# The first attention chunk's scores: products in the layout of the projection, summed over the head dimension by column-tiled matmuls

## The chip, the cores and the metric

The kernel runs on one core of a Trainium2 chip. The metric is the device time of the core in microseconds (us). A profile's own span is about 1.8 us shorter than the time of the same execution. Engines: TensorE (PE in the profile; PEld is its weight loads), VectorE (DVE), ScalarE (ACT), GpSimd (POOL), SyncE (SP).

Before the change: 777.38 us, the median of three executions (777.25 to 777.75).

## The reference

One transformer block on 2048 rows of 1024 features. Cut to what matters:

```python
def attention_part(x, wqkv, wo):           # H = 32 heads of Dh = 32, window W = 8, dilation 2
    q, k, v = split_heads(x @ wqkv)
    idx = pos[:, None] - 2 * arange(8)      # each position sees itself and 7 earlier ones, two apart
    logits = einsum("bhsd,bhswd->bhsw", q, k[idx]) * Dh ** -0.5
    attn = softmax(where(idx >= 0, logits, -1e9))
    return merge_heads(einsum("bhsw,bhswd->bhsd", attn, v[idx])) @ wo

h  = x + attention_part(layernorm(x), wqkv, wo)
n  = layernorm(h)
h2 = h + ((n @ w_gate) * (n @ w_up)) @ w_down    # 3584 hidden features
```

## The kernel before

The rows are worked in four chunks of 512. For a chunk, TensorE computes q, k and v in 24 groups of eight matmuls of 512 columns (4 of 128 output features in each of six weight blocks: 0 and 1 are q, 2 and 3 k, 4 and 5 v). In that layout a partition is one feature, and the sum over the 32 features of a head runs across partitions; the additions of this kernel's VectorE all run along the free dimension. So each group's result goes to DRAM and is loaded again with a partition for every pair of a quarter of the chunk and a head:

```python
def evac_qkv(c, m, ps):
    sg = t1k.tile([128, HB + TC], BF, ...)
    nc.scalar.copy(sg[:, HB:HB + TC], ps[:])
    # ... the 14 earlier columns (the halo) for k and v ...
    nc.sync.dma_start(qd[c][...], sg[...])        # and kd, vd
```

Now the head's features lie along the free dimension, and the scores of two window positions are two products and a tree of halving adds:

```python
def attention(c):                                  # cut
    for wp in range(W // 2):
        for j in range(2):
            nc.vector.tensor_tensor(prod[:, j], qD[:], kD[:, :, o:o + SUB], ALU.mult)
            yield 2.3
        nc.vector.tensor_tensor(prod[:, :, 0:16], prod[:, :, 0:16], prod[:, :, 16:32], ALU.add)
        yield 2.3
        # ... 8, 4, 2, 1: five adds in all ...
    # ... mask, maximum, exponential, sum, reciprocal ...
    prefetch_qk(c + 1)
    while ("v", c) not in qkv_in:
        yield "later", 1.0
    # ... eight products with v ("pv") and their adds, then the store and reload of the output ...
```

The attention is a generator. A scheduler called after each matmul group decides how much of it is put into the program there. It is pure bookkeeping while the program is written, and does nothing on the chip:

```python
GROUP_US = 1.73
class Background:
    def spend(self, us):
        self.credit -= us
    def step(self, us):
        self.now += us
        self.credit = min(self.credit + us * self.rate, 4.0)
        while self.credit > 0:
            # take the first item that is ready; next(item) puts its next
            # instructions into the program and yields their cost
            self.credit -= got
```

The stretch that decides this case is the first output projection, `wo_ln2(0)`: eight groups of matmuls, whose results VectorE adds to the residual, with statistics and a normalisation for every 128 rows, which a DMA then transposes. Between it and the gate projection of the next part (`ffn1(0)`, tile `pg`), which reads all the transposed rows, lie eight groups of other work:

```python
    bg.finish(atts[0])
    bg.rate = 0.98
    nxt = wo_ln2(0)                       # per group: bg.spend(0.7 ...); bg.step(GROUP_US)
    qkv(3, range(4, 6), last=True)        # eight groups
    start_attention(3)
    lnT2, hs = nxt
    hT = ffn1(0, lnT2)                    # pg, pu
```

The order at the start of the program:

```python
    qkv(0, range(1, 4))
    load_qk(0)
    # ...
    start_attention(0)                    # ready 16 us later
    qkv(1, range(4))
    qkv(0, range(4, 6))
    load_v(0)
```

## Time and profile before

| | before |
|---|---|
| time, median of 3 | 777.38 us |
| span of the profiled execution | 774.8 us |
| TensorE busy | 768.9 us (99%) |
| VectorE busy | 612.0 us (79%) |
| TensorE's waits | 2.5 us, of which 2.1 before the first projection |

The table says that TensorE has almost no room: it is busy for 768.9 of 774.8 us. The author's estimate from this is that an added matmul makes the program longer by what it occupies, unless it falls into a wait, and that work taken off another engine makes it hardly shorter. The prediction below shows the rows. One more pair of rows is useful as the "before" of two comparisons. The first fence is TensorE in order of time (start, us, engine, line, operation, tiles, count) around the first output projection of the kernel before; the second is its DMA view of the 16 us in which the rows of a later chunk are transposed, as GB/s in 40 slices of 0.4 us.

```profile
163.33 13.98 PE L515 MATMUL wo<-w_wo,oT 128*128 128x512 bf16 x64
190.96 1.89 PE L394 MATMUL pg<-lnT,w_wg 128*128 128x512 bf16 x8
```

```profile
GB/s 314 348 344 346 293 296 288 291 288 291 288 292 293 288 289 287 276 155 261 281 291 238 217 206 169 220 204 181 179 207 202 144 216 209 154 205 206 201 150 219
```

The gate projection begins 27.6 us after the output projection, with 16 groups of 1.73 us between them: no wait. The transposes move 144 GB/s or more in every slice.

### The profile page before, as it was taken

Reading aid. Unit: us, or ns where it says so; the run is one execution under the profiler, and the core shown is the slowest. Engines: PE = TensorE matmul, PEld = TensorE weight load, DVE = VectorE, ACT = ScalarE, POOL = GpSimd, SP = SyncE. Lnnn points to the kernel's source line nnn. Section 1 sums busy time; section 2 is a strip of 40 time slices with the busy share of each in tenths; the row PEclk is TensorE's granted clock in tenths of the full one; section 3 lists DMA queues with packets and bytes.
Section 4 is the critical chain, followed back from the end, with each engine's and each line's share of the span. In section 5 each row is a group of like instructions: output and inputs, shape, how many; then the busy total and the mean of one; then the engine's idle time right before and its main releaser. Section 6 shows DMA issues by size and latency. Waiting matters only on the chain.

```text
span 774.8 us, 10428 instructions
## 1 busy us (share of the span) xinstructions
PE 768.9 (99%) x3691; PEld 353.5 (46%) x3691; DVE 612.0 (79%) x782; ACT 471.3 (61%) x1021; POOL 142.1 (18%) x152
## 2 busy tenths in 40 slices
PE   8999999999999999999999999999999999999998
PEld 6444444444444444444444444444444444444444
DVE  5629999999899999999988989985553444578863
ACT  4627534323476661975869899746677776788240
POOL 0000000010000200002000001008778687600000
PEclk9999999999999999999999999999999999999999
DMA  8998693895965868876745375644332423740001
GB/s 285 262 267 194 160 288 86 259 287 145 342 204 167 269 226 242 263 231 229 240 138 195 129 271 150 158 100 111 108 93 71 109 59 105 241 140 28 0 28 55
DMA packets 183716, 134.38 MB, mean 173 GB/s; under 512 B 81264, under 2 KB 176496, under 8 KB 181616
## 3 DMA queue, kind: packets, MB, share of 16 engines
q1 hardware_dynamic: 176912, 110.12, 49.9%
q0 software_dynamic: 3584, 22.02, 8.2%
q10 hardware_dynamic: 3168, 1.57, 0.9%
q8 instruction: 29, 0.48, 0.3%
q14 instruction: 23, 0.19, 0.1%
HBM read 104.86 MB, written 22.02 MB: 164 GB/s over the span
## 4 chain that ended last, share of the span: by engine, by line
PE 86%; DVE 9%; DMA 2%; ACT 1%; SPq 1%; issue 0%; DVEq 0%
PE ps L394 18%; PE pu L394 12%; PE pg L394 12%; PE dx L790 6%; PE pz L683 6%; PE acc L629 6%; PE py L683 6%; PE px L683 6%; PE wo L515 4%; PE pv L683 3%; PE dy L790 3%; DMA x<-in_A_x_dram 2%; DVE st L181 1%; DVE h L837 1%; PE ps L355 1%; PE ex L790 1%
## 5 line engine op out<-in xcount | busy, mean ns | idle before, releaser
L394 PE MATMUL ps<-lnT,w_qkv 128*128 128x512 bf16 x736 | 159.7, 379 | 0.2 <-ACT sg L307 0.2
L394 PEld LDWEIGHTS <-w_qkv 128*128 128x128 bf16 x736 | 71.8, 98 | 86.6 <-issue 0.7
L394 PE MATMUL pg<-lnT,w_wg 128*128 128x512 bf16 x448 | 105.8, 379 | 0.0
L394 PE MATMUL pu<-lnT,w_wu 128*128 128x512 bf16 x448 | 105.8, 379 | 0.0
L307 ACT CAST sg<-ps 128x512 bf16<-128x512 f32 x96 | 54.7, 590 | 51.3 <-PE ps L394 49.9
L477 DVE TENSOR_TENSOR pv<-vD,at 128x4096 bf16<-128x4096 bf16 x32 | 72.5, 2286 | 0.3
L434 DVE TENSOR_TENSOR prod<-qD,kD 128x4096 bf16<-128x4096 bf16 x32 | 72.3, 2284 | 0.1
L683 PEld LDWEIGHTS <-sw 128*128 128x128 f16 x448 | 43.8, 98 | 53.5 <-issue 0.9
L394 PEld LDWEIGHTS <-w_wu 128*128 128x128 bf16 x448 | 43.9, 98 | 52.8
L394 PEld LDWEIGHTS <-w_wg 128*128 128x128 bf16 x448 | 43.8, 98 | 52.7
L599 ACT CAST us<-pu 128x512 bf16<-128x512 f32 x56 | 33.2, 592 | 40.3 <-PE pu L394 39.5
L683 PE MATMUL px<-lnT,ws 128*128 128x512 bf16 x224 | 55.2, 379 | 0.0
L683 PEld LDWEIGHTS <-ws 128*128 128x128 f16 x336 | 32.9, 98 | 39.6
L629 PE MATMUL acc<-w_wd,gs 128*128 128x512 bf16 x224 | 48.5, 379 | 0.0
L489 POOL DMA_DIRECT2D od<-oD x4 | 2.2, 542 | 251.4 <-DVE oD L487 162.5
L664 POOL TENSOR_TENSOR sw<-ws 128x512 f16<-128x512 f16 x26 | 29.9, 1150 | 84.8 <-PE py L683 77.5
L185 ACT ACTIVATE rs<-mv,eps 128x1 f32<-128x1 f32 (+1 forms) x25 | 7.4, 297 | 53.5 <-DVE mv L182 48.6
L594 ACT CAST gs<-pg 128x512 bf16<-128x512 f32 x56 | 32.8, 586 | 10.7 <-PE pg L394 8.7
L436 DVE TENSOR_TENSOR prod<-prod 128x4096 bf16<-128x4096 bf16 x16 | 36.6, 2289 | 0.3
L543 ACT ACTIVATE junkd<-w_wd 128x512 bf16<-128x512 bf16 x56 | 34.3, 613 | 0.0
L629 PEld LDWEIGHTS <-gs 128*128 128x128 bf16 x224 | 21.9, 98 | 26.4
L700 ACT COPY py<-px 128x512 f32<-128x512 f32 x28 | 16.0, 570 | 26.3 <-PE px L683 26.3
(312 smaller groups left out, 1390.7 us busy)
## 6 DMA issues: line engine op xcount, KB each, us to landing
w_wg<-in_B_w_gate_dram SPq DMA_DIRECT2D x14, 1024.0 KB, 6.9
w_wu<-in_B_w_up_dram SPq DMA_DIRECT2D x14, 1024.0 KB, 5.4
w_wd<-in_B_w_down_dram SPq DMA_DIRECT2D x8, 896.0 KB, 7.7
w_pair<-in_B_w_gate_dram SPq DMA_DIRECT2D x14, 512.0 KB, 4.0
w_pair<-in_B_w_up_dram SPq DMA_DIRECT2D x14, 512.0 KB, 5.3
w_wo<-in_A_wo_dram SPq DMA_DIRECT2D x6, 1024.0 KB, 8.3
w_qkv<-in_A_wqkv_dram SPq DMA_DIRECT2D x5, 1024.0 KB, 11.0
kd<-sg SPq DMA_DIRECT2D x32, 144.0 KB, 3.3
```

What stands on the lines that cost most here:

```text
L307: nc.scalar.copy(sg[:, HB:HB + TC], ps[:])
L394: nc.tensor.matmul(ps[:], lhsT=wt[:, ko, bass.ts(j, 128)], rhs=rhs[:, ko, :], start=(ko == 0), stop=(ko == KO - 1))
L434: nc.vector.tensor_tensor(prod[:, j], qD[:], kD[:, :, o:o + SUB], ALU.mult)
L436: nc.vector.tensor_tensor(prod[:, :, 0:16], prod[:, :, 0:16], prod[:, :, 16:32], ALU.add)
L477: nc.vector.tensor_tensor(pv[:, j], vD[:, :, o:o + SUB], at[:, w, None, :].to_broadcast((128, DH, SUB)), ALU.mult)
L515: nc.tensor.matmul(ps[:], lhsT=oTs[c][:, kk, t, :], rhs=wts["wo", c, hf][:, kk, :], start=(kk == 0), stop=(kk == KO - 1))
L543: nc.scalar.activation(junk, src, ACTF.Abs, accum_out=self.l1[:, k:k + 1])
L594: nc.scalar.copy(gs[:], pg[:])
L599: nc.scalar.copy(us[:], pu[:])
L629: nc.tensor.matmul(acc[t][:], lhsT=hT[f][:, bass.ts(t, 128)], rhs=wts["wd", c, hf, b][:, j, :], start=(f == 0), stop=(f == NF - 1))
L683: nc.tensor.matmul(ps[:], lhsT=lhs[:, ko, :], rhs=rhs[:, ko, :], start=(fresh and ko == 0), stop=(ko == 3), skip_group_check=not fresh)
L790: nc.tensor.matmul(ps[:, bass.ds(lo, n)], lhsT=lhs[k][:, bass.ts(q, 128)], rhs=rhs[k][:, bass.ds(lo, n)], start=(fresh and k == 0), stop=( ...
```

## The change

For chunk 0 alone, the trip through DRAM is left out. q and k stay in the layout of the projection (`qT`, `kT`). VectorE multiplies them there, two groups of heads and four window positions in one instruction, and the sum over a head's 32 features is done by TensorE: a matmul with a weight of 128 x 32 zeros and ones adds up the partitions of each head. Its weight has 32 columns where the ordinary ones have 128 (128*32 and 128*128 in the traces), so four such matmuls, one for each quarter of the chunk, are sent to four different column tiles (quarters of the array's columns). The result lands in the layout that the rest of the attention expects. The intent is to start chunk 0's attention some 20 us earlier and to take the adding tree off VectorE. The order of the weight blocks and of the first projections is changed so that a half of q and of k are there early. Core of the diff, with cuts marked:

```diff
+NAT = (3, 2, 1, 0, 7, 6, 5, 4)
-    for b in range(6):
+    for b in (0, 2, 1, 3, 4, 5):
         stream.append((("qkv", b), wqkv_v[:, :, bass.ts(b, 512)], KO))
 # ... mask in the order NAT; "heads": the 0/1 weights; tiles qT, kT ...
     def evac_qkv(c, m, ps):
+        if c == 0 and m < 16:
+            natural.add(m)
+            # ... copy ps into qT or kT (and the halo), no DMA ...
+            return
+    def natural_logits(lg):
+        # ... four product buffers; acc: two PSUM tiles ...
+        def reduce(i):
+            for g in range(2):
+                hg = i // 2 * 2 + g
+                for cp in range(4):
+                    rows = slice(32 * cp, 32 * cp + 32)
+                    nc.tensor.matmul(acc[i % 2][rows], lhsT=heads[:, hg, :],
+                                     rhs=bufs[i % 4][:, g, :, bass.ts(cp, SUB)],
+                                     start=(hg == 0), stop=(hg == KO - 1))
+        for i in range(8):
+            # ... wait until the four groups that are needed are in "natural" ...
+            nc.vector.tensor_tensor(bufs[i % 4], qT[...].to_broadcast((128, 2, 4, TC)), win, ALU.mult)
+            yield 2.3
+            if i > 1:
+                reduce(i - 2)
+        yield "later", 2.0
+        reduce(6)
+        nc.scalar.copy(lg[:, 0:4], acc[0][:])
+        yield "later", 2.0
+        reduce(7)
+        nc.scalar.copy(lg[:, 4:8], acc[1][:])
 # ... attention(c): logits(c, lg) for c > 0, natural_logits(lg) for c == 0 ...
-        bg.add(atts[c], bg.now + (16.0 if c == 0 else 0.0))
-    qkv(0, range(1, 4))
-    load_qk(0)
+        bg.add(atts[c], bg.now)
+    qkv(0, (2,))
+    start_attention(0)
+    qkv(0, (1, 3))
```

More of the change, by code (lines that the diff above doesn't have):

```diff
@@ L295 @@
     nc.gpsimd.memset(mask[:], 0.0)
-    for w in range(1, W):
-        nc.gpsimd.memset(mask[:, w, 0:DIL * w], NEG)
+    for i, w in enumerate(NAT):
+        if w:
+            nc.gpsimd.memset(mask[:, i, 0:DIL * w], NEG)
+    heads = t1k.tile([128, KO, 32], BF, tag="t1k", name="heads")
+    nc.gpsimd.memset(heads[:], 0.0)
+    for i in range(4):
+        base = heads[32 * i:32 * i + 32, 0, i:i + 1]
+        nc.gpsimd.memset(bass.AP(base.tensor, base.offset, [list(base.ap[0]), [36, KO]]), 1.0)
+    qT = att.tile([128, KO, TC], BF, tag="qD", name="qT")
+    kT = att.tile([128, KO, HB + TC], BF, tag="kD", name="kT")
+    nc.gpsimd.memset(kT[:, :, 0:HB], 0.0)
+    natural = set()
     wps = psum.tile([128, 512], F32, tag="mm", name="warm_ps")
@@ L305, in evac_qkv @@
     def evac_qkv(c, m, ps):
+        if c == 0 and m < 16:
+            natural.add(m)
+            if m < 8:
+                nc.scalar.copy(qT[:, m, :], ps[:])
+            else:
+                nc.scalar.copy(kT[:, m - 8, HB:HB + TC], ps[:])
+                nc.scalar.copy(halo[:, m - 8, :], ps[:, TC - HB:TC])
+            return
         sg = t1k.tile([128, HB + TC], BF, tag="t1k", name=f"sg{c}_{m}")
@@ L425, in prefetch_qk, with logits @@
             load_qk(c)
-    def attention(c):
+    def natural_logits(lg):
+        room = att.tile([128, 2, 2, 4, TC], BF, tag="prod", name="nprod")
+        bufs = [room[:, 0], room[:, 1], att.tile([128, 2, 4, TC], BF, tag="oD", name="nprod_o")[:],
+                att.tile([128, 2, 4, TC], BF, tag="vD", name="nprod_v")[:]]
+        acc = [psum.tile([128, 4, SUB], F32, tag="mm", name=f"lgp{i}") for i in range(2)]
+        def reduce(i):
[3 more added lines that the diff above has]
+                    rows = slice(32 * cp, 32 * cp + 32)
+                    nc.tensor.matmul(acc[i % 2][rows], lhsT=heads[:, hg, :], rhs=bufs[i % 4][:, g, :, bass.ts(cp, SUB)],
+                                     start=(hg == 0), stop=(hg == KO - 1))
+        for i in range(8):
+            hg = i // 2 * 2
+            while not {hg, hg + 1, hg + 8, hg + 9} <= natural:
+                yield "later", 1.0
+            base = kT[:, hg, HB - DIL * (i % 2 * 4 + 3):HB]
+            win = bass.AP(base.tensor, base.offset, [list(base.ap[0]), [HB + TC, 2], [DIL, 4], [1, TC]])
+            nc.vector.tensor_tensor(bufs[i % 4], qT[:, hg:hg + 2, None, :].to_broadcast((128, 2, 4, TC)), win, ALU.mult)
+            yield 2.3
[7 more added lines that the diff above has]
+        nc.scalar.copy(lg[:, 4:8], acc[1][:])
+    def logits(c, lg):
         qD, kD = qkv_in["q", c], qkv_in["k", c]
-        lg = att.tile([128, W, SUB], F32, tag="lg", name=f"lg{c}")
         for wp in range(W // 2):
@@ L445, in attention @@
             yield 1.0
+    def attention(c):
+        lg = att.tile([128, W, SUB], F32, tag="lg", name=f"lg{c}")
+        order = range(W) if c else NAT
+        yield from logits(c, lg) if c else natural_logits(lg)
         if c == 0:
@@ L475, in attention @@
                 w = 2 * wp + j
-                o = HB - DIL * w
+                o = HB - DIL * order[w]
                 nc.vector.tensor_tensor(pv[:, j], vD[:, :, o:o + SUB],
@@ L739 @@
     bg.add(stats_gen(norm1[3]), bg.now + 6.0)
-    start_attention(0)
     qkv(1, range(4))
```

## The prediction

> **What bounds the kernel now.** I read the page's busy shares first, then TensorE's own waits, then the chain that ended last, then the order of time on VectorE. The page (engine, busy us, share, instructions):
>
> ```profile
> PE 768.9 (99%) x3691; PEld 353.5 (46%) x3691; DVE 612.0 (79%) x782; ACT 471.3 (61%) x1021; POOL 142.1 (18%) x152
> ```
>
> Busy can flatter pipelined matmuls, so I asked TensorE's list of waits (total us, times, longest us). All of it:
>
> ```profile
> PE warm_ps L301 <- DVE warm L287: 1.2, 1, 1.2
> PE pt L349 <- DVE ln L342: 0.6, 1, 0.6
> PE ps L355 <- ACT lnT L350: 0.3, 1, 0.3
> PE ps L394 <- ACT sg L307: 0.2, 1, 0.2
> PE pv L683 <- DVE h L795: 0.2, 1, 0.2
> ```
>
> TensorE waits 2.5 us in 774.8, and 2.1 of that lies before the first projection. The chain of waits (start, us, what) shows its pace and the stretch that will matter:
>
> ```profile
> 59.74 103.76 PE ps L394 x480
> 163.50 13.81 PE wo L515 x64
> 177.31 13.81 PE ps L394 x64
> 191.12 1.73 PE pg L394 x8
> ```
>
> 103.76 us over 480 matmuls is 216 ns each, though the groups show 379 ns for one: matmuls overlap, and 216 ns is the price of one more in the queue. The granted clock is 1.00 in every stretch I asked. So time is the number of TensorE slots plus its waits. Taking work off VectorE or the DMA queues saves at most the 0.2 us waits.
>
> VectorE's chain for one pair of chunk 0's window positions, in order of time (start, us, instruction):
>
> ```profile
> 59.96 4.45 DVE L434 TENSOR_TENSOR prod<-qD,kD 128x4096 bf16<-128x4096 bf16 x2
> 64.44 2.29 DVE L436 TENSOR_TENSOR prod<-prod 128x4096 bf16<-128x4096 bf16 x1
> 66.77 1.22 DVE L438 TENSOR_TENSOR prod<-prod 128x2048 bf16<-128x2048 bf16 x1
> 68.03 1.22 DVE L441 TENSOR_TENSOR t<-prod 128x1024 f32<-128x1024 bf16 x1
> 69.28 0.69 DVE L443 TENSOR_TENSOR t<-t 128x512 f32<-128x512 f32 x1
> 70.01 0.43 DVE L444 TENSOR_TENSOR lg<-t 128x256 f32<-128x256 f32 x1
> ```
>
> And the first output projection, where VectorE is late:
>
> ```profile
> 171.27 2.29 DVE L436 TENSOR_TENSOR prod<-prod 128x4096 bf16<-128x4096 bf16 x1
> 173.48 1.28 DVE L517 TENSOR_TENSOR h<-wo,h 128x512 bf16<-128x512 f32 x2
> ...
> 186.34 0.55 DVE L190 TENSOR_SCALAR ln<-h,mv,rs 128x1024 bf16<-128x1024 bf16 x1 [0.60 <-ACT rs L186]
> ```
>
> The first wo tile is on TensorE from 163.3, its add runs at 173.48; the last normalised rows are done at 186.89, their transpose lands about 3.1 us after its issue (tile lnT), near 190, and the gate projection that reads it starts at 191.0 without a wait. That chain has 1 us of slack or less.
>
> [...] No instruction of this trace is column-tiled[...]. [...] a product with a broadcast middle dimension already costs 2286 ns here (pv, L477), against 2284 ns for prod (L434).
>
> **The change part by part.**
>
> Removed: for chunk 0, 16 stores and two loads (q, k) through DRAM, and on VectorE four times the tree (2.29 + 1.22 + 1.22 + 0.69 + 0.43 = 5.85 us), 23.4 us. None is on TensorE's path: worth 0. Kept: eight products of 4096 elements, about 2.29 us each, now started near 39 us, where VectorE idles from 39.0 to 54.3.
>
> Added on TensorE: 8 reductions of 2 head groups x 4 column tiles = 64 matmuls of 512 columns, in eight separate bursts between ordinary groups. If four tiles run together, a burst is 2 rounds x 216 = 432 ns. [...] I choose 0.8 us a burst (0.45 to 1.05): 6.4 us. All of it lies on the bound.
>
> Waits for the products: following the kernel's own scheduler by its credits, reduction i is issued two products later, near 42, 46.5, 49 us and on; products end near 41.3, 43.6, 45.9 and every 2.3 us. TensorE finds them ready, by 0.7 us for the first. [...] The old 0.2 us wait at 59.7 came from ScalarE stuck behind statistics of x that landed at 54.3; these are now issued after the products, and the x loads have a freer queue, so I take that wait off: -0.2.
>
> A new wait: the attention generator runs 21 us ahead in the order of issue but VectorE executes no earlier against TensorE at wo. Its first pv now waits for v of chunk 0, whose load can't be issued before the v projections are stored (84.23 before, 5.5 us to land): about 89.6 plus the added TensorE time s. From there, with durations of before: rest of chunk 0, 34.4 (111.48 to 145.88); four score pairs of chunk 1, 41.8 (59.96 to 103.55, less 1.8 of x norms between); maximum to exponential 3.9; sum and reciprocal 2.5; at 1.2. Sum 173.4 + s for the first wo add, against 173.48: the same lateness. But the scheduler's credit now stands at -0.99 on entering wo, instead of -1.34; after the first tile's -0.70 + 1.73 it is +0.04, so one pv product of 2.28 us is put among the adds (before: -0.31, none). The last norm then comes 2.28 later relative to TensorE, -0.1 for the start, +0.2 for the missing wait, less a slack of 0 to 1: TensorE waits about 1.9 us before the gate projection.
>
> Sum: 777.4 + 6.4 + 1.9 - 0.2 = 785.5; I put 785.3, as rival (b) below is likelier than (c).
>
> **Rivals.**
>
> (a) The column tiles don't overlap. Then 64 x 216 = 13.8 us[...]: near 793 with the wo wait, just at the 2% limit (792.9). [...] For it: nothing in this trace shows tiles together. I give it 0.13.
>
> (b) No wait at wo: v lands early enough, or slack is larger: 783.5. For it: the estimate rests on sums of 90 us in which 1 us decides, and v's load may take less than 5.5 us. 0.35.
>
> (c) A larger wait: VectorE or ScalarE late in the reduction stage[...], or v landing late (the other v loads show up to 10.9 us), which would move the wo wait one for one and bring 788 to 791. 0.15.
>
> (d) The freed VectorE time shortens the kernel. The waits list allows at most 0.5 us of this. 0.01.
>
> **Range and chances.** Overlapping tiles without and with the wait give 781.0 (8 x 0.45) to 788; serial tiles or a late v reach 791 to 794. So 781 to 791.5 at 8 in 10; faster 0.01, within 2% 0.88, slower 0.11.
>
> **What would show it.** Right: new TensorE matmuls of 512 columns and 32 weights in eight bursts of about 0.8 us, their starts within a burst far closer than 216 ns; TensorE's waits list with one new entry of 1 to 3 us, at the first gate matmul (pg), released by the transpose; one pv between the first wo adds; no tree on VectorE in chunk 0. Wrong: starts 216 ns apart in a burst (rival a); a wait at a reduction for its product[...] (c); a span that is shorter with no wait removed.

## The result, and the profile after

| | before | after |
|---|---|---|
| time, median of 4 | 777.32 us | 788.76 us (787.24 to 790.25) |
| ratio | | 1.0146 (95%: 1.0132 to 1.0160) |
| span of the profiled execution | 774.8 us | 785.5 us |

A ratio here and below is the mean time of one kernel's runs over the mean of the other's runs of the same rounds, so it is not quite the ratio of the medians. 788.76 lies within the predicted range of 781.0 to 791.5, but 3.5 us above the predicted 785.3. The profiled execution of before was among the shortest seen (executions of it span 774.8 to 776.1), so differences of half a microsecond in the 10.7 between the spans aren't read further.

First the work that was taken away. The page after has for TensorE and the others (busy us, share, instructions):

```profile
PE 772.2 (98%) x3695; PEld 354.0 (45%) x3755; DVE 590.1 (75%) x762; ACT 472.8 (60%) x1015; POOL 142.0 (18%) x156
```

VectorE lost 21.9 us of work and 20 instructions. TensorE has 64 matmuls more, not the 4 that the page shows: 60 of its matmul records are missing here (the repeated run below lists all 3755, as many as weight loads). In the view by stretches, from 60 to 104 us, VectorE's busy time fell from 43.21 to 15.71 us while TensorE was busy 44.00 and 43.79 of 44.00 us: the freed time bought nothing.

Now what was added. TensorE in order of time, after:

```profile
42.71 0.61 PE L457 MATMUL lgp<-nprod,heads 128*32 128x512 bf16 x8
43.26 3.63 PE L413 MATMUL ps<-lnT,w_qkv 128*128 128x512 bf16 x16
46.81 0.61 PE L457 MATMUL lgp<-nprod,heads 128*32 128x512 bf16 x8
...
168.70 14.20 PE L569 MATMUL wo<-w_wo,oT 128*128 128x512 bf16 x63
...
199.61 1.89 PE L413 MATMUL pg<-lnT,w_wg 128*128 128x512 bf16 x8 [2.85 <-DMA lnT<-ln]
...
529.31 1.02 PE L737 MATMUL pv<-prodx,sw 128*128 128x512 f16 x4 [2.06 <-DVE h L849]
```

A burst of eight reductions begins at 42.71 and the next ordinary matmul at 43.26: 0.55 us for eight matmuls of 512 columns, where eight ordinary ones take 1.73. Between the ordinary start at 43.26 and the next burst at 46.81 lie 3.55 us, and 16 ordinary matmuls at 216 ns are 3.45: another 0.10. A burst costs 0.65 us, eight of them 5.2. No bracket at a burst: TensorE never waits for a product. The brackets at `pg` and at the late `pv` are two new waits. The list of TensorE's waits (total us, times, longest us) agrees:

```profile
PE pg L413 <- DMA lnT<-ln: 2.9, 1, 2.9
PE pv L737 <- DVE h L849: 2.3, 2, 2.1
```

Set against the same landmarks of before, the delay grows like this:

| landmark | before | after | delay |
|---|---|---|---|
| first group of 512 columns | 17.02 | 17.55 | 0.53 |
| first output projection | 163.33 | 168.70 | 5.37 |
| gate projection after it | 190.96 | 199.61 | 8.65 |
| second output projection | 287.65 | 296.30 | 8.65 |
| first `pv` of the later part | 518.67 | 529.31 | 10.64 |
| end | 774.8 | 785.5 | 10.7 |

The 10.7 us are therefore 5.2 of bursts less 0.4 of an old wait and its gap (before, the 152 matmuls from 26.54 to 59.74 took 33.2 us, and 152 x 216 ns are 32.8), 0.5 at the start, 2.85 of the wait at `pg` with 0.4 of small gaps in the output projection and behind it, and 2.1 at `pv`.

The wait at `pg` can be followed back on VectorE, in order of time:

```profile
37.30 4.49 DVE L466 TENSOR_TENSOR nprod<-qT,kT 128x4096 bf16<-128x4096 bf16 x2
...
96.88 4.50 DVE L531 TENSOR_TENSOR pv<-vD,at 128x4096 bf16<-128x4096 bf16 x2 [19.52 <-DMA vD<-vd]
...
180.71 0.68 DVE L571 TENSOR_TENSOR h<-wo,h 128x512 bf16<-128x512 f32 x1
181.31 2.28 DVE L531 TENSOR_TENSOR pv<-vD,at 128x4096 bf16<-128x4096 bf16 x1
183.51 0.68 DVE L571 TENSOR_TENSOR h<-wo,h 128x512 bf16<-128x512 f32 x1
```

The first line is the new product, 4.49 us for two, where two of the other layout took 4.45 before. VectorE then has its scores early, and at 77 us nothing to do: it waits 19.52 us for v, whose load was issued at 89.7 and took 7.1. From there on it is busy but for one wait of 1.1 us for ScalarE, and comes to the first residual add at 180.71, 12.0 us after the output projection began (10.2 before). Then one `pv` product of 2.28 us stands between the first two adds, which wasn't there before. The last rows are normalised from 195.76 to 196.31, their transpose lands 3.1 us after its issue, and the gate projection starts at 199.61; TensorE had been free for it since 196.8.

Beside this, three of the four executions after had a mean granted clock below 1.000: 0.998, 0.995 and 0.998, with spans of 786.9, 788.5 and 787.1, against 785.5 at 1.000. That is where the median lost another 1.5 us to the profiled execution.

### The profile page after: what moved, and what is told of

It is laid out like the page before. It is cut to its first block, busy times and chain, and to the rows that moved or that the text cites. A ratio compares the mean times of both kernels' runs of the same rounds, so it can differ in the third digit from the quotient of the medians.

```text
span 785.5 us, 10418 instructions
## 1 busy us (share of the span) xinstructions
PE 772.2 (98%) x3695; PEld 354.0 (45%) x3755; DVE 590.1 (75%) x762; ACT 472.8 (60%) x1015; POOL 142.0 (18%) x156
## 4 chain that ended last, share of the span: by engine, by line
PE 79%; DVE 15%; DMA 3%; ACT 1%; issue 1%; ACTq 0%; DVEq 0%
PE pg L413 12%; PE pu L413 12%; PE ps L413 8%; PE dx L844 6%; PE pz L737 6%; PE acc L683 6%; PE py L737 6%; PE px L737 6%; PE wo L889 3%; PE pv L737 3%; PE dy L844 3%; DVE pv L531 3%; DVE prod L483 2%; PE wo L569 2%; PE ex L844 2%; DVE prod L485 1%
## 5 line engine op out<-in xcount | busy, mean ns | idle before, releaser
L326 ACT CAST sg<-ps 128x512 bf16<-128x512 f32 x80 | 46.9, 588 | 64.6 <-PE ps L413 62.9
L483 DVE TENSOR_TENSOR prod<-qD,kD 128x4096 bf16<-128x4096 bf16 x24 | 54.4, 2285 | 0.1
L737 PE MATMUL px<-lnT,ws 128*128 128x512 bf16 x212 | 53.1, 379 | 0.6
L654 DVE TENSOR_TENSOR gs<-gs,us 128x512 bf16<-128x512 bf16 x56 | 23.5, 419 | 24.7 <-ACT us L653 24.5
L683 PEld LDWEIGHTS <-gs 128*128 128x128 bf16 x224 | 21.9, 98 | 26.4
L737 PE MATMUL pv<-prodx,sw 128*128 128x512 f16 x112 | 28.7, 379 | 2.3 <-DVE h L849 2.3
```

Source lines behind the costliest of these rows:

```text
L683: nc.tensor.matmul(acc[t][:], lhsT=hT[f][:, bass.ts(t, 128)], rhs=wts["wd", c, hf, b][:, j, :], start=(f == 0), stop=(f == NF - 1))
L737: nc.tensor.matmul(ps[:], lhsT=lhs[:, ko, :], rhs=rhs[:, ko, :], start=(fresh and ko == 0), stop=(ko == 3), skip_group_check=not fresh)
```

## The experiments

**Theory.** The bursts cost what they occupy. The `pg` wait comes from the order of issue (one product let in by credit) and from the late v. The late `pv` wait and the clock were not foreseen and have no reason yet. **Rivals:** the tiles don't overlap and something else became shorter; the whole loss is chip-to-chip scatter; the late wait is a consequence of the changed kernel's delay and not of its instructions.

Four experiments of three rounds, on one chip (before: 777.07).

**The changed kernel again, unaltered.**

> The changed kernel again, unaltered, for its spread and for which of its four extra costs return in a second profile (bursts 5.2 us, first-gate wait 2.9, wait at the first pv of the last stage 2.1, start 0.5). If all four belong to the change: ratio to before 1.013 to 1.016, the waits list again shows about 2.9 us at pg and about 2.1 at pv. Rival: the 2.1 and the 0.5 are chance of that one execution; then they are under 0.5 here and the span is 783 to 784.

788.13 us (786.19 to 788.39), ratio 1.0137. Both waits came back (2.8 at `pg`, and at `pv` a longest of 1.4, against 2.1), and three of four executions again had a clock of 0.998. The first group began at 17.18 instead of 17.55, so 0.2 to 0.5 us at the start is scatter. The rest repeats.

**Keep the product out by credit alone.**

```diff
     bg.rate = 0.98
+    bg.spend(0.1)
     nxt = wo_ln2(0)
```

> Changed kernel with 0.1 us of scheduler credit taken before the first output projection, so that its credit stays below zero and no pv product lands among the wo adds. My theory: one pv of 2.28 us is what made the last norm late; the wait at the first gate matmul falls from 2.9 to 0.3-0.9 us and the span by about 2.3. Rival (VectorE is late anyway, because v landed late, and the pv only fills a hole): the wait stays near 2.9 and the span unchanged.

784.69 us, ratio 1.0097. TensorE's wait list now has

```profile
PE pg L413 <- DMA lnT<-ln: 0.7, 1, 0.7
```

A tenth of a microsecond of bookkeeping moves one product and takes 2.1 us off the wait, with the same instructions executed, one of them later. The median fell by 3.4, more than the wait: the clock was 1.000, 0.999, 1.000, 1.000.

**Load v earlier.** The v projections of chunk 0 and their load are put ahead of chunk 1's q and k (and the refill of the weight stream that they need ahead of that):

```diff
     xtiles[2] = load_x(2, "x", nc.sync)
+    pump(6)
# ...
     xtiles[3] = load_x(3, "x", nc.sync)
-    pump(6)
     bg.add(stats_gen(norm1[3]), bg.now + 6.0)
-    qkv(1, range(4))
     qkv(0, range(4, 6))
     load_v(0)
+    qkv(1, range(4))
```

> Changed kernel with chunk 0's v projections moved ahead of chunk 1's q and k (and their weights loaded earlier), so that v of chunk 0 can be loaded some 28 us earlier. If VectorE's lateness at wo comes from its 19.5 us wait for v: that wait shrinks below 3 us, VectorE reaches the first wo add 6 us or more earlier against TensorE, the wait at pg is 0 and the span falls by 2.9 to 3.3 although a product is still put among the wo adds. Rival (lateness set by the number of VectorE instructions): pg still waits over 2 us. Risk: the fifth and sixth weight blocks come late and TensorE waits near 40 us.

783.30 us, ratio 1.0080; all clocks 1.000. There is no wait at `pg`. The first `pv` product ran at 75.30 without a wait, and the first residual add came 3.8 us after the output projection's start, not 12.0. VectorE still has one attention add between the residual adds, and it no longer matters. So the wait at `pg` has two causes, the product let in and the late v, and removing either all but ends it. The wait at `pv` stayed at 1.8.

**No column tiles.** The same 64 matmuls, with 0/1 weights of 128 columns that put each quarter on its own output rows, all accumulated over the full array:

```diff
-                    nc.tensor.matmul(acc[i % 2][rows], lhsT=heads[:, hg, :], rhs=bufs[i % 4][:, g, :, bass.ts(cp, SUB)],
-                                     start=(hg == 0), stop=(hg == KO - 1))
+                    nc.tensor.matmul(acc[i % 2][:], lhsT=heads[hg][:, cp, :], rhs=bufs[i % 4][:, g, :, bass.ts(cp, SUB)],
+                                     start=(hg == 0 and cp == 0), stop=(hg == KO - 1 and cp == 3))
```

> Changed kernel with the same 64 reduction matmuls at full width: 0/1 weights of 128 columns, zero outside the tile's own 32, no column tiles. If the four column tiles really run together: bursts grow from 0.55 to 1.7 us (8 x 216 ns), less about 0.1 each[...], so the span rises by 7.5 to 9 us against the changed kernel. If the tiles were not what makes the burst short: no difference over 1 us.

795.79 us, ratio 1.0242 (slower). TensorE in order of time:

```profile
18.30 7.07 PE L414 MATMUL ps<-lnT,w_qkv 128*128 128x512 bf16 x32 [0.84 <-DMA w_qkv<-in_A_wqkv_dram]
...
43.37 1.89 PE L457 MATMUL lgp<-nprod,heads 128*128 128x512 bf16 x8
45.09 3.62 PE L414 MATMUL ps<-lnT,w_qkv 128*128 128x512 bf16 x16
```

From 43.37 to 45.09 is 1.72 us for eight: 215 ns each, one after the other. This span of 793.9 is 9.5 us longer than the repeated run's 784.4, more than the 7.5 to 9 expected. The bursts are 8.6 of it: 160 ordinary matmuls and the eight bursts take 48.34 us here (27.83 to 76.17) and 39.74 in the repeated run (26.70 to 66.44). Most of the rest is a later start, 18.30 for 17.18, with a new wait of 0.84 us for weights. So the column tiles overlap. The 48.34 us are 216 ns for each of 224 matmuls: eight bursts at full width have no cost beside their matmuls, and the 0.10 us that a tiled burst adds to the work behind it goes with the tiles.

The second call (before: 777.23) went after the late wait. What is late there is ScalarE: it normalises rows into buffers that the program gives it again when the transpose of earlier rows has landed, then scales weights, and VectorE's result `h` and the `pv` matmuls come after that. In the kernel after, ScalarE waits twice for the transposes, 2.6 us in all; in the kernel before, not at all. The DMA view of those 16 us, after, has GB/s by slice and the queues (packets, MB, share):

```profile
GB/s 348 347 343 306 289 284 293 292 298 285 298 297 289 293 290 272 179 21 68 281 291 288 236 208 189 196 227 17 3 9 67 279 292 289 278 238 175 127 216 205
...
q8 instruction: 1, 0.02, 0.4%
q14 instruction: 1, 0.01, 0.2%
```

In two places the transposes all but stop, near 509 and near 513 us, for some 0.6 and 1.4 us, and in these 16 us two fetches of instructions fall (queues of kind "instruction"), one of queue 14 between 505 and 506 and one of queue 8 between 512 and 513. In the same stretch of before there is no fetch and no stop. Over the whole run, queue 8 has 29 fetches, 0.48 MB in all. TensorE executes 3755 weight loads and as many matmuls, 7510 instructions, which is one fetch for every 259 (in the kernel before 2 x 3691 and 29 fetches, one for every 255). The change adds 64 matmuls and 64 weight loads, 128 instructions, to TensorE and takes 20 from VectorE, so later fetches come at other moments. The author's estimate, from the one fetch for every 255 to 259 instructions: if fetches follow the count of an engine's instructions, then another 128 on TensorE, 256 with those of the change, shift its fetches by about one whole interval and so bring them back to where they were, and 20 on VectorE restore its old count. If the wait belongs to the delay or to the new order, neither will.

**128 more instructions on TensorE** (on top of the early v): the 13 warm-up matmuls of 512 columns are cut into 77 of 86, which should leave the warm-up its length. It took 5.57 us with the 13, 4.93 in this run with the 77, and 5.56 in the run below that has both shifts.

```diff
-    for i in range(13):
-        nc.tensor.matmul(wps[:], lhsT=warm[:, 0:128], rhs=warm[:], start=True, stop=True)
+    for i in range(77):
+        nc.tensor.matmul(wps[:, 0:86], lhsT=warm[:, 0:128], rhs=warm[:, 0:86], start=True, stop=True)
```

> The early-v version, with the 13 warm-up matmuls of 512 columns replaced by 77 of 86 columns: the same array time before the first data, but 128 TensorE instructions more, so that with the 128 of the reductions TensorE's instruction stream is 256 longer than before. Theory: the remaining 1.8-2.0 us wait at the first pv of the last stage comes from instruction fetches that now fall among the row transposes of chunks 2 and 3 (one near 501, one near 507-510 in every run of the change, none there before); the later one is TensorE's. Then it leaves that stretch, the wait falls to about 0.9 us and the span by about 1. Rival (the wait comes from the change's lighter VectorE or DMA load, not from fetches): wait still 1.8 to 2.0.

782.18 us, ratio 1.0061. The longest wait at `pv` fell from 1.8 to 0.5, and in the stretch of the transposes only the fetch of queue 14 is left. ScalarE's wait for the transposes fell from 2.2 us (twice) to 1.0 (once).

**20 more on VectorE** (on top of the early v):

```diff
+    pad = const.tile([128, 20], F32)
+    for i in range(20):
+        nc.vector.memset(pad[:, i:i + 1], 0.0)
```

> The early-v version with 20 tiny memsets of separate columns added to VectorE before the first data, so that VectorE's instruction stream is as long as before (the change takes 20 off). Theory: the earlier of the two fetches, near 501, is VectorE's and leaves the stretch; the wait at the first pv falls from 1.8-2.0 to 1.0-1.5. Rival (not VectorE's stream, or not fetches): the fetch stays where it is and the wait at 1.8 to 2.0.

782.75 us, ratio 1.0069. Only the fetch of queue 8 is left, ScalarE waits 1.1 us once, and the longest wait at `pv` is 1.3. In the DMA records of the traces, these 20 instructions move 7 of queue 14's 23 fetches by more than 2 us (the one at 501.5 to 486.9) and none of queue 8's; the 128 on TensorE move every fetch of queue 8 and one of queue 14, by 2 us. So queue 8 serves TensorE, and queue 14 serves VectorE among others. The 1.3 us alone would prove little: with both fetches in the stretch, the longest wait at `pv` is 1.3 to 2.1 in the six traces that have them.

**Both.**

> Both shifts on the early-v version. Theory: no fetch among the transposes, wait at the first pv back to 0.2-0.4 us as before the change, span 779.7 to 780.2, so only the bursts (5.2 us) remain of the change. Rival: wait 1.8 to 2.0, span 781.5.

781.96 us, ratio 1.0059 (1.0042 to 1.0076). No fetch is left in the stretch, ScalarE doesn't wait for the transposes, and TensorE's list has what it had before the change (0.2 also in the three later runs that keep the fetches away):

```profile
PE pv L741 <- DVE h L852: 0.2, 1, 0.2
```

So 64 more matmuls, their 64 weight loads and 20 memsets, none of which the result needs, make the kernel 1.3 us faster than the version with the early v alone (in another call; against each call's own before, 1.0059 for 1.0080).

**The control: the same 128 in the kernel before**, which has none of the change.

> The kernel before with the 77 small warm-up matmuls, that is 128 TensorE instructions more and nothing else changed. Theory: TensorE's fetch now falls among the transposes in this kernel too and the wait at the first pv grows from 0.2 to 1.0-1.5 us, the time by about 1 us. Rival (fetch position does not matter): wait 0.2, time within 0.3 us of before.

778.15 us, ratio 1.0009 (0.9994 to 1.0024): as a time, not told apart from before. The trace does tell it apart. The wait list and the DMA view of the transposes:

```profile
PE pv L683 <- DVE h L795: 1.8, 2, 1.5
```

```profile
GB/s 343 332 291 291 288 292 291 291 289 288 293 289 292 276 230 165 280 292 277 215 209 192 176 205 13 3 10 53 281 290 290 278 266 172 110 216 205 156 220 209
...
q8 instruction: 1, 0.02, 0.4%
```

One fetch of queue 8, one stop of 1.4 us, and a wait of 1.5 us at `pv` where before had 0.2. The rival that tied the late wait to the delay of the changed kernel falls.

The third call (before: 777.76; one round, on the base of the version with both shifts) was on the price of a burst.

**Same tile first.** Within a burst the two matmuls of one tile come one after the other (tiles 0, 0, 1, 1, ...) and not in turn (0, 1, 2, 3, 0, ...).

```diff
-            for g in range(2):
-                hg = i // 2 * 2 + g
-                for cp in range(4):
+            for cp in range(4):
+                for g in range(2):
+                    hg = i // 2 * 2 + g
```

> The version with early v and both shifts, with the eight matmuls of a burst in the order tile by tile (both head groups of one column tile in succession) instead of group by group (four different tiles in succession). If matmuls start in program order and only neighbours on different tiles overlap, a burst takes about 5 x 216 = 1.1 us instead of 0.55 and the span grows by 8 x 0.5 = 4 us. If the array sorts out the order by itself: burst still 0.55, span unchanged.

```profile
42.39 0.62 PE L461 MATMUL lgp<-nprod,heads 128*32 128x512 bf16 x8
42.95 3.63 PE L417 MATMUL ps<-lnT,w_qkv 128*128 128x512 bf16 x16
```

781.91 us, span 779.9, against 780.0 with the tiles in turn. A burst took 0.56 us, against 0.54. The 1.1 us that I had expected, for the case that only neighbours on different tiles overlap, didn't come: the order of the tiles made no difference in bursts of eight.

**Every reduction twice**, with weights of one half. It adds 64 matmuls and 64 weight loads, so the cut warm-up is undone and the fetches stay where they were.

```diff
# ... the ones in "heads" become 0.5 ...
-                for cp in range(4):
+                for n in range(8):
+                    cp = n % 4
                     # ... start only for n < 4, stop only for n > 3 ...
```

> Early v and VectorE's shift, with every reduction matmul issued twice at weights of 0.5, so a burst has 16 matmuls in four rounds (and the 128 extra TensorE instructions keep the fetch away from the transposes). If a round of four tiles costs one slot of 216 ns[...]: a burst grows by 0.43 to 0.98 us, the span by 8 x 0.43 = 3.5 against the version with both shifts. If the cost is mostly fixed: under 1.5.

```profile
42.37 1.05 PE L462 MATMUL lgp<-nprod,heads 128*32 128x512 bf16 x16
43.35 3.63 PE L417 MATMUL ps<-lnT,w_qkv 128*128 128x512 bf16 x15
```

785.07 us, span 783.3. A burst of 16 takes 0.98 us, so eight more in four tiles cost 0.44, or 0.22 for a round of four: a round of four tiles costs what one full matmul does. Eight times 0.44 is 3.5; the span grew by 3.3. The remainder of a burst of 0.65, after two rounds of 0.216, is 0.22. The bursts at full width had no such remainder, so I take it for a fixed price of a tiled burst. What it consists of isn't shown.

**Four bursts of 16 for eight of 8.** If the 0.22 us is the price of a burst, four fewer save 4 x 0.22 = 0.9 us.

```diff
-            if i > 1:
+            if i > 2 and i % 2:
+                reduce(i - 3)
                 reduce(i - 2)
# ... and reduce(6), reduce(7) together at the end ...
```

> Early v and both shifts, with the reductions issued two at a time: four bursts of 16 instead of eight of 8. Theory: a burst costs 0.65 us of which 0.43 are its two rounds[...]; four bursts fewer save 4 x 0.22 = 0.9 us of the 5.2, span 779.1. Rival: the 0.22 is weight loading per round and does not go: span unchanged at 780.0.

780.81 us, ratio 1.0038 (1.0009 to 1.0067), span 779.0: 0.9 less than with eight bursts (779.9, the order tile by tile). This is the best version of the change that I found, and its interval still lies above 1.

**The clock.** In the last (before: 777.39) the kernel after has 12 matmuls whose result nobody reads in the place of the wait at `pg`, to ask whether the idle of TensorE is what lowers the clock.

```diff
     lnT2, hs = nxt
+    keep = psum.tile([128, TC], F32, tag="mm", name="keep")
+    for i in range(12):
+        nc.tensor.matmul(keep[:], lhsT=ident[:], rhs=wts["wg", 0, 0][:, i % KO, :], start=True, stop=True)
     hT = ffn1(0, lnT2)
```

> The changed kernel with 12 idle matmuls (result unused, 12 x 216 = 2.6 us) put just before the first gate projection, where TensorE otherwise waits 2.9 us. The gate still starts when its transpose lands, so the time of an execution at full clock stays 786 to 787. Theory: the executions with a granted clock of 0.998 and 0.995 and 2 to 4 us more come from that idle stretch; filled, nearly all executions show 1.000 and the median is 786 to 787 with a spread under 1 us. Rival (the clock dips are of another cause): clocks of 0.998 in more than half of the executions and a median near 788.5 as before.

```profile
196.55 2.75 PE L814 MATMUL keep<-w_wg,ident 128*128 128x512 bf16 x12
199.57 1.67 PE L413 MATMUL pg<-lnT,w_wg 128*128 128x512 bf16 x7 [0.26 <-DMA lnT<-ln]
```

786.80 us (786.41 to 786.95), ratio 1.0123. The gate projection starts when it did (199.57 for 199.61), but all four executions are at 1.000, with spans of 784.6 to 785.2. Of the eight executions of the kernel after with the idle, six were below. Over the kernels, by the idle in their profiled execution: with 2.8 or 2.9 us idle, six of eight at 0.998 or less; with 2.4 us (no column tiles), one of four at 0.998; with no idle over 1.9 us after the start-up (all others, before included), none below 0.999. Two of these, with the credit taken and with the early v, ran on the chip of the repeat. So the lowered clock goes with the idle (six of eight executions below 1.000 with it, none of four with it filled), and filling it with useless work is worth 1.3 us against the repeat and 2.0 against the first result. All profiled executions were at 1.000, so no trace shows the idle of a lowered one, or where in it the clock fell.

## Why the prediction was right or wrong

**The bound and the value of what was removed: right.** 21.9 us of VectorE work (23.4 had been counted) and the q and k trips of chunk 0 were worth nothing. With everything else mended (both shifts, early v) the kernel is still 1.0059 of before: only the bursts are left.

**Rival (a), tiles one after another: refuted** by the kernel without column tiles, which is what that rival would have been (1.72 us a burst, 795.79 us; the rival's figure was near 793).

**The burst: rounds right, the rest too large.** Predicted 0.8 us a burst, 6.4 in all; measured 0.65 and 5.2. The two rounds of 216 ns were right: the doubled reductions show 0.22 us a round. The term that failed was what the prediction allowed beyond the rounds, 0.8 - 0.43 = 0.37 us, which was the author's estimate and not shown by the trace before: 0.22 us pays for all of it, and bursts at full width pay none.

**No wait for the products: right.** No burst waits, and the predicted wait of 0.2 us that was to disappear did.

**The wait at the gate projection: mechanism right, size too small.** The credit arithmetic that lets one product in came true to the instruction, and the run in which 0.1 of credit is taken away shows that it is the cause. Predicted 1.9 us, measured 2.85 with 0.4 of gaps. The term that was mis-sized is "5.5 us to land": v took 7.1, so the first residual add came not at the same lateness, as the sum of 173.4 + s said, but 1.9 later (12.0 for 10.2 us; 1.6 of it is the landing). The loads of q and k for chunk 1 were issued at 90.4 and 90.9, right behind v at 89.7, where before v had no other load of this kind beside it; whether they slowed it was not tested. Product and lateness are 2.28 + 1.9 = 4.2 us; the wait and the gap behind the output projection took about 3.3 of this, so the slack was about 0.9, within the 0 to 1 that was allowed. Rival (c) named the late load of v, and was in part what happened; its other half, VectorE or ScalarE late in the reduction stage, didn't: no wait stands there. What the 0.4 of gaps is stays open; in two later runs (the credit taken, the wait filled) TensorE waits 0.3 and 0.4 us inside the output projection for a ScalarE copy.

**Missing altogether: the late wait, 2.1 us.** No step of the prediction looked beyond the gate projection. A change in the number of instructions moved a fetch of TensorE's and one of VectorE's into a stretch in which DMA transposes are on the path. Shown by moving them out, one by one and both, and by moving one into the kernel before. How a fetch stops the transposes isn't shown. In the DMA records each fetch in this stretch has one stop: for queue 8 it begins within 0.8 us of the fetch and lasts 1.0 to 1.6, for queue 14 it begins 3.5 to 3.8 us after it and lasts 0.4 to 0.6.

**Missing: the granted clock, about 1.5 us.** The prediction counted a wait at its length. Where the profiled execution waits 2.8 or 2.9 us, the six others, all below a clock of 1.000, took 1.4 to 3.0 us more than it.

The sum was 8.1 us over before; the profiled span is 10.7 over, and the difference is -1.2 (bursts) + 0.95 and 0.4 (the `pg` wait and its gaps) + 0.5 (start, scatter) + 2.1 (late wait) - 0.2 (the old wait's gap) = +2.55, of the 2.6 between them. Misses of opposite sign, and the range was wide enough for terms that were not in it: that the number came near is in part luck. The chance of "same" was right because the bound was.

## What to carry to other kernels

In a kernel bound by TensorE, price a change by the TensorE slots and the idle that it adds, whatever it takes off the other engines; and after any change of issue order, follow the scheduler's arithmetic through the next stretch in which an engine is late, since one product there cost 2.1 us of wait, as much as three bursts. Fewer, longer bursts of tiled matmuls save the fixed price of a burst (0.9 us for four fewer). When a wait appears far from the edit (2.1 us here), look whether an instruction fetch has moved into it, and try to fill an idle of TensorE near 3 us if it can't be removed (filling 2.8 to 2.9 us was worth 1.3 us here).

## What the runs showed of the hardware

- Instruction fetches: 29 of queue 8 for 7510 TensorE instructions, one for every 259, 0.48 MB in all; the 23 of queue 14, which serves VectorE among others, have 0.19 MB, 8.3 KB each. A fetch among DMA transposes went with a stop of nearly all transfers (0.4 to 1.6 us), and the stops cost about a microsecond (medians: 783.30 to 781.96 us with two fetches moved away; 777.23 to 778.15 with one moved into the kernel before, where the interval of the ratio includes 1).
- Granted clock: a kernel whose two profiled executions idle 2.8 and 2.9 us had a mean granted clock of 0.995 to 0.998 in six of eight executions, and a time 1.4 to 3.0 us longer; with the gap filled, four of four were at 1.000. The six have no trace, and a longer idle in them isn't excluded. The mean doesn't show how far the clock was lowered, or for how long.
- Column tiles: four of 32 columns cost 0.22 us a round, the same as one full matmul (0.216), and the order of the tiles within a burst of eight made no difference (0.56 for 0.54 us).
- A tiled burst between matmuls of 512 columns at full width cost 0.22 us beyond its rounds, and four bursts fewer took 0.9 us less. What the 0.22 us consists of isn't shown.
